# Turning the keys of units 6 and later: one whole-tile stream transpose and 16 transfers inside SBUF in place of 16 small transposes

## The chip, the cores and the metric

The kernel runs on one core of a Trainium2 chip. The metric is the device time of one launch in microseconds; the figure of a kernel is the median of several launches. A core has five engines that each work through a queue of their own in order: TensorE (PE, with its weight loads shown apart as PEld), VectorE (DVE), ScalarE (ACT), GpSimd (POOL) and SyncE (SP). SP computes nothing here: it issues nearly all the DMAs.

## The reference

Two blocks follow each other. The first is a gated linear recurrence over 4 batches, 8 heads, 768 steps, head width 48; the second is a maxout feed-forward network on the 3072 tokens that come out, 384 features wide, with 768 inner features.

```python
f = 1.0 / (1.0 + np.exp(-f_logit))
for t in range(S):
    state = f[:, :, t, :, None] * state + np.einsum('bhd,bhe->bhde', k[:, :, t], v[:, :, t])
    y[:, :, t] = np.einsum('bhd,bhde->bhe', q[:, :, t], state)
x = y.transpose(0, 2, 1, 3).reshape(B * S, H * D)
h = np.maximum(np.maximum(x @ w1, x @ w2), x @ w3)
out = h @ w_out
```

## The kernel before, in words

The recurrence is done in chunks of 64 steps (`C`). A **unit** is one chunk of two batches: 128 token rows (`UT`), eight heads of 48 features padded to 64 (`DP`). There are 24 units (`NU`), numbered `u`; two neighbouring units are the two batch pairs of the same chunk. Four units (`GRP`) make a group of 512 tokens on which the feed-forward network runs. All arithmetic is fp32.

For each unit the kernel makes `kh`, the keys scaled by what the gates leave of them until the chunk's end, and `qh`, the scaled queries, both with features on the partitions (two heads stacked, 2 x 64) and tokens along the row. `pairs(u)` multiplies keys with queries inside the chunk, `values(u)` and `finish(u)` make the outputs, and `sums(u)` (line 437) makes the chunk's contribution to the state: 16 matrix products whose stationary operand is the keys with **tokens** on the partitions, `ks`, and whose moving operand is the values. So `kh` has to be turned into `ks`.

Units 0 to 5 (`BY_ROWS` is 6) are turned on TensorE (`keys`, lines 371 and 373). Units 6 to 21 are turned on VectorE by `keys_by_blocks` (line 386): 16 stream transposes a unit, each of a 32-partition strip with 4 blocks of 32x32. They are issued in four portions of four, two at the end of one pass of the main loop and two in the next.

The rest of a unit's chain, in VectorE's order: `scan(n)` turns the gates (line 300) and runs a scan over them (`r`, line 333); `after(n)` turns the loaded keys into the tile `kt` (line 300, one buffer) and POOL multiplies them with `r` into `kh` (line 344); `before(n)` runs the second scan (`prod`, line 351), turns the queries into `qt` and POOL makes `qh` (line 355).

The order of all instructions is the order in which the code is written (`tc.manual_schedule()`); the framework adds the waits. The main loop runs over `u`. In one pass, with `n = u + 1`, the products of the feed-forward network stand in five portions (`fill(part)`), each a fifth of a unit's share of TensorE work. Between them stand, in this order: `values(u - 1)` and `sums(u - 1)`, `pairs(u)`, `finish(u - 1)`; `pack` (line 528), two DMAs inside SBUF that close up a group's features, in passes where `u % 4` is 3 or 0; loads; `scan(n)`; [portion] `after(n)`, `before(n)`; [portion] `carry(n)`; [portion] the turning of unit `n`'s keys; [portion] `check_load` (line 273), one weight piece loaded again for a check on its range.

SP's queue therefore holds, in the order of the code: loads of `f`, `k`, `q` by `load` (line 187, eight DMAs for each of the three for two units together), of `v` by `load_v` (line 164, two a unit), moves of weights inside SBUF by `place` (lines 462 and 469), `pack`, `check_load`, and the stores of finished tokens (line 564, eight a group). Each DMA signals one of eight semaphores in turn (`DMAHW0` to `DMAHW7`) and waits until the DMA before it on the same one has landed.

Of the kernel before, what the change touches and what calls it, by code (L numbers as in the profile page):

```python
# [9 lines left out]
FP32 = mybir.dt.float32  # L10
# [36 lines left out]
C = 64  # L47
DP = 64
# [7 lines left out]
def kernel(  # L56
# [12 lines left out]
    nc = tc.nc  # L69
    B, H, S, D = q.shape  # L70
    HP = H // 2
    NU = B // 2 * (S // C)
    UT = 2 * C
# [16 lines left out]
    def fast():  # L90
        ctx = ExitStack()
        with ctx:
            work = ctx.enter_context(tc.tile_pool(name="work", bufs=2))
# [57 lines left out]
            BY_ROWS = 6  # L151
# [40 lines left out]
            def load_v(u, queues=one):  # L192
                load_tokens(v_tiles[u % NLD], v, u, queues)
# [109 lines left out]
            ready = {}  # L303
# [24 lines left out]
            def scan(u):  # L328
                gate = gate_tiles[u % 2]
                if u >= BY_ROWS:  # L330
                    turned(gate[:, :, 1:], ready[u])
                r = r_tiles[u % 2]
                nc.vector.tensor_tensor_scan(r[:, 0:LEN][:, ::-1], flat(gate)[:, ::-1], flat(from_one)[:, ::-1], 1.0,  # L333
                                             op0=ALU.mult, op1=ALU.max)
                whole = r[:, 0:LEN].rearrange("p (x t) -> p x t", t=C + 1)[:, :, 1]
                nc.vector.reciprocal(from_inv[u % 2][:, :, 0], whole)
# [28 lines left out]
            def keys(u):  # L365

                if u < min(BY_ROWS, NU - 2):
                    kh = ready[u]["kh"]
                    tr_s = ps_tr.tile([UT, HP, 128], FP32, name="tr")
                    for hp in range(HP):  # L370
                        nc.tensor.transpose(tr_s[:, hp, :], kh[:, hp].rearrange("p a t -> p (a t)"), ident)
                    ks = work.tile([UT, H, DP], FP32, name="ks")
                    nc.scalar.copy(ks.rearrange("s h d -> s (h d)"), tr_s.rearrange("s a d -> s (a d)"))
                    ready[u]["ks"] = ks

            def keys_by_blocks(u, n):

                if BY_ROWS <= u < NU - 2:
                    kh = ready[u]["kh"]
                    if n == 0:  # L380
                        ready[u]["ks"] = work.tile([UT, H, DP], FP32, name="ks")
                    ks = ready[u]["ks"].rearrange("s (hp par) d -> s hp par d", par=2)
                    a, t0 = divmod(n * 32, C)
                    for p0 in range(0, 128, 32):
                        par, e0 = divmod(p0, DP)
                        nc.vector.transpose(ks[n * 32:(n + 1) * 32, :, par, e0:e0 + 32], kh[p0:p0 + 32, :, a, t0:t0 + 32])  # L386

            FOUR = [(par, a) for a in range(2) for par in range(2)]

            def room_of_pairs():  # L390
                return ps_a.tile([128, 2, 512], FP32, name="a")
# [36 lines left out]
            def sums(u, p=None):  # L428

                d, v_ld = ready[u], v_tiles[u % NLD]  # L430
                if u < NU - 2:
                    d["sums"] = y = room_of_pairs() if p is None else p
                    Y = HP * C
                    for hp in range(HP):
                        for par, a in FOUR:
                            s = slice(a * C, (a + 1) * C)
                            nc.tensor.matmul(y[par * DP:(par + 1) * DP, a, Y + hp * D:Y + (hp + 1) * D],  # L437
                                             lhsT=d["ks"][s, 2 * hp + par, :], rhs=v_ld[s, 2 * hp + par, 0:D],
                                             start=True, stop=True)
                    if p is None:  # L440
                        new_state(u)

            def new_state(u):

                d = ready[u]
                if u < NU - 2:
                    ds = d["sums"][:, :, HP * C:HP * (C + D)]
                    new = states[u % 2].rearrange("p (a h) d -> p a (h d)", a=2)
                    if u < 2:
                        nc.scalar.copy(new, ds)  # L450
                    else:
                        nc.vector.tensor_tensor(new, ds, d["state"].rearrange("p (a h) d -> p a (h d)", a=2), op=ALU.add)
# [70 lines left out]
            def pack(u0, u1, xT, queues=one):  # L523

                t = slice(u0 * UT, (u1 + 1) * UT)
                for par in range(2):
                    p0 = par * DP
                    queues[par].dma_start(out=xT[p0 + D:p0 + DP, 0:NK, t], in_=xT[p0:p0 + D, NK, t])
# [447 lines left out]
            def fill(ns):  # L976
                budget[0] += ns
                while budget[0] > 0 and pending:
                    try:
                        budget[0] -= next(pending[0])  # L980
                    except StopIteration:
                        pending.pop(0)
# [18 lines left out]
            with tc.manual_schedule():  # L1001
# [80 lines left out]
                for u in range(GRP, NU):  # L1082
                    n = u + 1
                    part = EARLY if u < BY_ROWS else LATER if u < 2 * GRP else PART
                    if n == BY_ROWS:
                        scan(n)
                    fill(part)
                    keys_by_blocks(u, 2)
                    room_of_unit = room_of_pairs()
                    if u > GRP:  # L1090
                        values(u - 1)
                        sums(u - 1, room_of_unit)
                    keys(u)
                    pairs(u, room_of_unit)
                    if u > GRP:
                        finish(u - 1, xT)
                        if u % GRP == 3:
                            pack(0, 2, xT)
                        elif u % GRP == 0:
                            pack(3, 3, xT)  # L1100
                    if u % GRP == 0:
                        if u > GRP:
                            packed[u // GRP - 1] = xT
                            pending.append(ffn(u // GRP - 1, xT))
                        xT = x_tiles[u // GRP % 2]

                    if u + 2 <= BY_ROWS:
                        load(u + 2)
                    if u == BY_ROWS:
                        load(u + 2, one, "f")  # L1110
                    elif u + 1 != BY_ROWS and BY_ROWS <= u + 3 < NU and u % 2:
                        load(u + 3, one, "fkq" if u % GRP == 1 else "f")
                    if u + 2 < NU:
                        load_v(u + 2)
                    keys_by_blocks(u, 3)
                    if n < NU:
                        if n < BY_ROWS or n == BY_ROWS + 2:
                            sigmoids(n)
                        if n != BY_ROWS:
                            scan(n)  # L1120
                    fill(part)
                    if n < NU:
                        after(n)
                        before(n)
                    if u == 2 * GRP:
                        mix_in(2, nc.vector)
                    check_range(u - CHECKS, 0)
                    fill(part)
                    if BY_ROWS < u + 2 < NU and u % GRP == 0:
                        load(u + 2, one, "k")  # L1130
                    if u == BY_ROWS:
                        load(u + 2, one, "kq")
                    if n < NU:
                        carry(n)
                    else:
                        values(u)
                    check_range(u - CHECKS, 1)
                    fill(part)
                    if BY_ROWS < u + 2 < NU and u % GRP == 0:
                        load(u + 2, one, "q")  # L1140
                    if u == 2 * GRP:
                        for part_of in range(2 * NK + 2):
                            place(w_lin, w_nat, part_of)
                    if n == NU:
                        finish(u, xT)
                        pack(3, 3, xT, both)
                        packed[u // GRP] = xT
                    keys_by_blocks(n, 0)
                    fill(part - 1000 if u < 2 * GRP else part)
                    keys_by_blocks(n, 1)  # L1150
                    check_range(u - CHECKS, 2)
                    if u + 2 >= CHECKS:
                        check_load(u + 2 - CHECKS)
                    if BY_ROWS <= u + 2 < NU and u != BY_ROWS:
                        sigmoids(u + 2)
# [269 lines left out]
```

## Time and profile before

| | |
|---|---|
| device time, median of 3 (lowest, highest) | 406.77 us (406.07, 406.93) |
| span of the profiled execution | 403.7 us |
| PE / PEld busy | 390.9 us (97%) / 339.7 us (84%) |
| DVE busy | 297.7 us (74%) |
| POOL / ACT busy | 256.4 us (64%) / 180.9 us (45%) |
| DMA, mean | 117 GB/s, 181611 packets |
| SP's DMA issues | 423 |

The page of the profile gives each engine's busy time; issuing a DMA is not counted as busy, so SP has no row among them, and its work is read from the timeline of its own queue and from its waits. The profile has no other time for this execution than the span; the median of the launches lies 3.1 us above it. In the rows of groups, the numbers after the bar are busy time, mean duration in ns and the idle time of the engine ahead of them.

### The profile page before, as it was taken

Reading aid. Unit: us, or ns where it says so; the run is one execution under the profiler, and the core shown is the slowest. Engines: PE = TensorE matmul, PEld = TensorE weight load, DVE = VectorE, ACT = ScalarE, POOL = GpSimd, SP = SyncE. Lnnn points to the kernel's source line nnn. Section 1 sums busy time; section 2 is a strip of 40 time slices with the busy share of each in tenths; the row PEclk is TensorE's granted clock in tenths of the full one; section 3 lists DMA queues with packets and bytes.
Section 4 is the critical chain, followed back from the end, with each engine's and each line's share of the span. In section 5 each row is a group of like instructions: output and inputs, shape, how many; then the busy total and the mean of one; then the engine's idle time right before and its main releaser. Section 6 shows DMA issues by size and latency. Waiting matters only on the chain.

```text
span 403.7 us, 11683 instructions
## 1 busy us (share of the span) xinstructions
PE 390.9 (97%) x4658; PEld 339.7 (84%) x4658; DVE 297.7 (74%) x572; ACT 180.9 (45%) x431; POOL 256.4 (64%) x283
## 2 busy tenths in 40 slices
PE   5988999999999999999999999999999999999995
PEld 4766765559998889998889988899988889988995
DVE  6997897999989999897998997998995450002600
ACT  3478787422224442345532344523354425586120
POOL 2189695879997697296587277667477850435700
PEclk9999999999999999999999999999999999999999
DMA  8999986767574576576635477634573003541002
GB/s 171 233 282 284 279 214 89 153 92 150 82 96 114 69 154 135 104 120 84 131 104 97 62 113 88 156 78 81 75 157 91 1 19 87 143 136 70 2 19 63
DMA packets 181611, 47.21 MB, mean 117 GB/s; under 512 B 160497, under 2 KB 179249, under 8 KB 181553
## 3 DMA queue, kind: packets, MB, share of 16 engines
q1 hardware_dynamic: 177536, 45.52, 54.7%
q10 hardware_dynamic: 4016, 0.91, 1.1%
q8 instruction: 37, 0.61, 0.6%
q14 instruction: 22, 0.17, 0.1%
HBM read 37.75 MB, written 4.72 MB: 105 GB/s over the span
## 4 chain that ended last, share of the span: by engine, by line
PE 90%; SPq 4%; DMA 1%; ACT 1%; issue 1%; POOL 1%; DVE 0%
PE p L884 20%; PE p L633 18%; PE tr L884 16%; PE tr L633 14%; PE p L546 7%; PE y L419 3%; PE p L787 3%; PE a L400 2%; PE y L508 2%; PE a L437 2%; SPq L178 2%; DMA v_ld<-in_v_dram 1%; SPq L164 1%; SPq L222 1%; PE tr L295 1%
## 5 line engine op out<-in xcount | busy, mean ns | idle before, releaser
L386 DVE STREAM_TRANSPOSE ks<-kh 32x128 f32<-32x128 f32 x256 | 77.5, 303 | 11.5 <-POOL kh L344 7.4
L884 PE MATMUL tr<-xT,placed 128*128 128x256 f32 x180 | 44.4, 384 | 0.0
L343 POOL COPY ends<-r 128x8 f32<-128x8 f32 x24 | 8.6, 358 | 48.1 <-DVE r L333 48.1
L884 PEld LDWEIGHTS tr<-xT,placed 128*128 128x128 f32 x180 | 33.5, 190 | 4.9
L344 POOL TENSOR_TENSOR kh<-kt,r 128x512 f32<-128x512 f32 x18 | 31.9, 1772 | 8.5 <-DVE kt L300 8.5
L333 DVE TENSOR_TENSOR_SCAN r<-gate,from_one 128x520 f32<-128x520 f32 x24 | 33.2, 1382 | 5.4 <-ACT gate L312 2.8
L546 PE MATMUL p<-xT,w_in 128*128 128x256 f32 (+1 forms) x108 | 33.9, 458 | 3.0 <-POOL w_in L756 1.9
L597 POOL TENSOR_TENSOR w_in<-hm 128x256 f32<-128x256 f32 x18 | 13.3, 737 | 32.2 <-DVE hm L935 29.4
L515 ACT COPY xT<-y 64x256 f32<-64x256 f32 (+1 forms) x60 | 22.1, 368 | 22.4 <-PE y L508 21.7
L351 DVE TENSOR_TENSOR_SCAN prod<-gate,from_inv 128x520 f32<-128x520 f32 x24 | 31.6, 1317 | 0.0
L884 PE MATMUL tr<-xT,w_in 128*128 128x256 f32 x120 | 30.8, 379 | 0.0
L641 DVE TENSOR_TENSOR o<-tr,w_in 128x384 f32<-128x384 f32 (+1 forms) x11 | 5.7, 521 | 33.4 <-PE tr L633 29.0
L884 PE MATMUL p<-w_in,placed 128*128 128x256 f32 x120 | 30.4, 382 | 0.0
L633 PE MATMUL p<-placed,hm 128*128 128x192 f32 x144 | 29.7, 333 | 0.0
L546 PEld LDWEIGHTS p<-xT,w_in 128*128 128x128 f32 x108 | 19.5, 190 | 12.0 <-issue 6.0
L884 PE MATMUL p<-xT,placed 128*128 128x256 f32 x120 | 29.2, 379 | 0.0
L633 PE MATMUL tr<-w_out,w_in 128*128 128x192 f32 x144 | 28.6, 326 | 0.0
L927 DVE TENSOR_TENSOR hm<-tr,hm 128x512 f32<-128x512 f32 x15 | 10.3, 684 | 22.8 <-PE tr L884 15.9
L262 POOL TENSOR_TENSOR w_in<-top_bits,rest_bits 128x384 uint32<-128x384 uint32 x18 | 21.7, 1216 | 7.2 <-DVE top_bits L256 4.3
L884 PEld LDWEIGHTS p<-w_in,placed 128*128 128x128 f32 x120 | 22.4, 190 | 4.4 <-issue 1.5
L638 ACT COPY w_in<-p 128x384 f32<-128x384 f32 x15 | 7.2, 479 | 41.0 <-PE p L633 41.0
L284 ACT ACTIVATE raw<-top_bits 128x384 f32<-128x384 f32 x48 | 25.2, 526 | 0.4
(168 smaller groups left out, 995.6 us busy)
## 6 DMA issues: line engine op xcount, KB each, us to landing
raw<-in_moe_w_dram SPq DMA_DIRECT2D x24, 384.0 KB, 4.4
v_ld<-in_v_dram SPq DMA_DIRECT2D x48, 96.0 KB, 3.4
placed<-in_moe_w_dram SPq DMA_DIRECT2D x12, 384.0 KB, 6.3
out_dram<-o SPq DMA_DIRECT2D x45, 96.0 KB, 2.2
placed<-in_moe_w_out_dram SPq DMA_DIRECT2D x6, 384.0 KB, 5.4
f_ld<-in_f_logit_dram SPq DMA_DIRECT2D x36, 64.0 KB, 2.7
k_ld<-in_k_dram SPq DMA_DIRECT2D x36, 64.0 KB, 2.5
q_ld<-in_q_dram SPq DMA_DIRECT2D x36, 64.0 KB, 2.6
```

Of the source, the lines that this page charges most:

```text
L262: nc.gpsimd.tensor_tensor(dst, by(top), by(rest), op=ALU.add)
L284: nc.scalar.activation(over, size, AF.Relu, scale=(-1 / HI_MIN, 1.0)[step - 1], bias=(1.0, -HI_END * (1 - 2.0 ** -24))[step - 1], accum_ou ...
L333: nc.vector.tensor_tensor_scan(r[:, 0:LEN][:, ::-1], flat(gate)[:, ::-1], flat(from_one)[:, ::-1], 1.0, op0=ALU.mult, op1=ALU.max)
L344: (nc.vector if u < BY_ROWS else nc.gpsimd).tensor_tensor(kh.rearrange("p h a t -> p a h t"), kt, by_batch(r[:, 1:LEN + 1].rearrange("p (x ...
L351: nc.vector.tensor_tensor_scan(flat(prod), flat(gate_tiles[u % 2]), flat(from_inv[u % 2]), 1.0, op0=ALU.mult, op1=ALU.max)
L386: nc.vector.transpose(ks[n * 32:(n + 1) * 32, :, par, e0:e0 + 32], kh[p0:p0 + 32, :, a, t0:t0 + 32])
L419: nc.tensor.matmul(y[o:o + DP, a, hp * C:(hp + 1) * C], lhsT=v_ld[s, 2 * hp + par, :], rhs=d["at"][s, par, hp, :], start=(hp == 0), stop=F ...
L515: nc.scalar.copy(xT[o, :, t0 + a * C:t0 + (a + 1) * C], y[i, a, 0:HP * C].rearrange("p (h t) -> p h t", h=HP))
L546: nc.tensor.matmul(p if w < TOK else p.rearrange("p (two t) -> p two t", two=2), lhsT=w_in[i][:, kt, j * 128:(j + 1) * 128], rhs=x[:, t.st ...
L597: engine.tensor_tensor(dst, x, y, op=op)
L633: nc.tensor.matmul(b[:, p * HD:(p + 1) * HD], lhsT=x, rhs=w, start=id(b) not in begun, stop=True, skip_group_check=True)
L884: nc.tensor.matmul(b[:, j * HALF:(j + 1) * HALF], lhsT=w[:, (2 * n + j) * 128:(2 * n + j + 1) * 128], rhs=x, start=begin and j == 0, stop= ...
```

## The change

`keys_by_blocks` and its four calls a unit go. In their place stands `keys_by_rows`, called once a unit where the first portion stood. It turns the whole of `kh` by one stream transpose of 128 partitions into a tile of 32x32 blocks, whose elements are written 16 bytes apart so that the four head pairs lie innermost, and carries the 16 squares of 32 partitions x 128 elements (512 bytes a row) to their token rows in `ks` by 16 DMAs on SP's queue. The block tile is named `kt` with one buffer, the name and the buffer of the tile that `after` turns the loaded keys into. `sums` reads `ks` through `keys_of`: for units 6 and later a head's 64 features now lie 16 bytes apart.

```diff
-            def keys_by_blocks(u, n):
+            def keys_by_rows(u):
                 if BY_ROWS <= u < NU - 2:
                     kh = ready[u]["kh"]
-                    if n == 0:
-                        ready[u]["ks"] = work.tile([UT, H, DP], FP32, name="ks")
-                    ks = ready[u]["ks"].rearrange("s (hp par) d -> s hp par d", par=2)
-                    a, t0 = divmod(n * 32, C)
-                    for p0 in range(0, 128, 32):
-                        par, e0 = divmod(p0, DP)
-                        nc.vector.transpose(ks[n * 32:(n + 1) * 32, :, par, e0:e0 + 32], kh[p0:p0 + 32, :, a, t0:t0 + 32])
+                    by_32 = work.tile([128, HP * UT], FP32, name="kt", bufs=1)
+                    nc.vector.transpose(by_32.rearrange("p (n d h) -> p n h d", h=HP, d=32),
+                                        kh.rearrange("p h a (n t) -> p (a n) h t", t=32))
+                    ready[u]["ks"] = ks = work.tile([UT, H * DP], FP32, name="ks")
+                    for p in range(4):
+                        for n in range(4):
+                            nc.sync.dma_start(out=ks[n * 32:(n + 1) * 32, p * UT:(p + 1) * UT],
+                                              in_=by_32[p * 32:(p + 1) * 32, n * UT:(n + 1) * UT])
+
+            def keys_of(u, h):
+                ks = ready[u]["ks"]
+                if u < BY_ROWS:
+                    return lambda s: ks[s, h, :]
+                by_32 = ks.rearrange("s (par d hp) -> s par hp d", par=2, hp=HP)
+                return lambda s: by_32[s, h % 2, h // 2, :]
...
-                                             lhsT=d["ks"][s, 2 * hp + par, :], rhs=v_ld[s, 2 * hp + par, 0:D],
+                                             lhsT=keys_of(u, 2 * hp + par)(s), rhs=v_ld[s, 2 * hp + par, 0:D],
...
-                    keys_by_blocks(u, 2)
...
-                    keys_by_blocks(u, 3)
...
-                    keys_by_blocks(n, 0)
+                    keys_by_rows(n)
                     fill(part - 1000 if u < 2 * GRP else part)
-                    keys_by_blocks(n, 1)
```

SP's queue at units 6 and 7, before: the loads of values for two units, then the first move of weights (`placed`, here its first and last rows of a run), then the next loads.

```order
L164 DMA v_ld_128<-in_v_dram 64x8x48 x2
L164 DMA v_ld_129<-in_v_dram 64x8x48 x2
L462 DMA placed_134<-w_in_64 16x3x768 x2
L469 DMA placed_134<-w_in_64 48x768 x2
L469 DMA placed_134<-w_in_64 32x768
L469 DMA placed_134<-w_in_64 16x768
```

The same place in the changed program, whose line numbers are 8 higher from `keys_of` on.

```order
L164 DMA v_ld_128<-in_v_dram 64x8x48 x2
L164 DMA v_ld_129<-in_v_dram 64x8x48 x2
L386 DMA ks<-kt 32x128 x16
L470 DMA placed_134<-w_in_64 16x3x768 x2
L477 DMA placed_134<-w_in_64 48x768 x2
L477 DMA placed_134<-w_in_64 32x768
```

The 16 DMAs of unit 6 stand ahead of the move of weights and of every load behind it; 15 more such blocks follow, one in each unit up to 21.

DVE's queue from the turning of unit 7's keys to that of unit 8's, before (`at` and `st` belong to `pairs` and the state of earlier units, `gate` to the gates of the next); the rows are printed with what each waits for.

```order
L300 STREAM_TRANSPOSE kt<-k_ld_117 128x512
L351 SCALAR_TENSOR_TENSOR prod<-gate_100,from_inv_97 128x520 [waits DVE_49]
L300 STREAM_TRANSPOSE qt<-q_ld_119 128x512 [waits Pool_49]
L386 STREAM_TRANSPOSE ks<-kh 32x4x32 [waits Pool_49]
L386 STREAM_TRANSPOSE ks<-kh 32x4x32 x11
L403 TENSOR_TENSOR at<-a,mask 128x512 [waits PE_49]
L452 TENSOR_TENSOR st_141<-a,state 128x384
L386 STREAM_TRANSPOSE ks<-kh 32x4x32 x4
L300 STREAM_TRANSPOSE gate_99<-sig 128x8x64 [waits Activation_49]
```

The same stretch in the changed program.

```order
L300 STREAM_TRANSPOSE kt<-k_ld_117 128x512 [waits DMAHW4_49,DMAHW5_49,DMAHW3_49,DMAHW6_49,DMAHW2_49,DMAHW7_49,DMAHW1_49,DMAHW0_49]
L351 SCALAR_TENSOR_TENSOR prod<-gate_100,from_inv_97 128x520 [waits DVE_49]
L300 STREAM_TRANSPOSE qt<-q_ld_119 128x512 [waits Pool_49]
L381 STREAM_TRANSPOSE kt<-kh 128x4x4x32 [waits Pool_49]
L411 TENSOR_TENSOR at<-a,mask 128x512 [waits PE_49]
L460 TENSOR_TENSOR st_141<-a,state 128x384
L300 STREAM_TRANSPOSE gate_99<-sig 128x8x64 [waits Activation_49]
```

Sixteen rows of DVE have become one (line 381), and the turning of unit 7's loaded keys into `kt`, which waited for nothing (the loads of the two units of a pair were waited for at the first of them), now waits for the DMA semaphores of all eight lanes.

## The prediction

> **What bounds the kernel now.** I read the page first (busy shares, the chain that ended last), then the busy time of the stretch in which the change works, then SP's waits and SP's issue durations, since that queue has no busy row.
>
> ```profile
> PE 390.9 (97%) x4658; PEld 339.7 (84%) x4658; DVE 297.7 (74%) x572; ACT 180.9 (45%) x431; POOL 256.4 (64%) x283
> PE 90%; SPq 4%; DMA 1%; ACT 1%; issue 1%; POOL 1%; DVE 0%
> 75.00:300.00 225.00, 224.97 (x3027) 200.51 (x3025) 204.83 (x433) 87.30 (x213) 163.63 (x171) 1.00 0.61 106
> ```
>
> The last row is the stretch from 75 to 300 us, in which units 6 to 21 are turned: PE 224.97 of 225.00 us busy, DVE 204.83, ACT 87.30, POOL 163.63, granted clock 1.00. PE is the bound and waits for nothing there; DVE has 0% of the chain. Work taken off DVE can therefore bring PE forward by 0.03 us in this stretch at most.
>
> SP is the queue to which the change adds. Its waits from 75 to 295 us (total, times, longest), the rows of its own queue at both ends of the turning, and its issue durations (ns, lowest/median/highest):
>
> ```profile
> SPq L528 <- ACT xT L515: 31.6, 5, 7.4
> ...
> 70.48 1.32 SPq L462 DMA_DIRECT2D placed<-w_in  x2
> 71.84 5.69 SPq L469 DMA_DIRECT2D placed<-w_in  x8
> ...
> 258.49 0.53 SPq L273 DMA_DIRECT2D raw<-in_moe_w_dram  x1
> 259.12 1.40 SPq L164 DMA_DIRECT2D v_ld<-in_v_dram  x2
> 260.61 0.61 SPq L273 DMA_DIRECT2D raw<-in_moe_w_dram  x1
> ...
> 290.20 4.15 SPq L187 DMA_DIRECT2D q_ld<-in_q_dram  x8
> 294.39 0.49 SPq L273 DMA_DIRECT2D raw<-in_moe_w_dram  x1
> ```
> ```profile
> L469 SPq DMA_DIRECT2D placed<-w_in x16: 587/592/1226, 71.8 to 99.3; - x16
> L469 SPq DMA_DIRECT2D w_in<-w_in x8: 519/588/592, 122.3 to 127.0; - x8
> ...
> DMA to landing us min/median/max: 1.9/2.7/4.2
> ...
> L528 SPq DMA_DIRECT2D xT<-xT x19: 556/613/1336, 99.9 to 334.2; - x19
> ...
> L187 SPq DMA_DIRECT2D f_ld<-in_f_logit_dram x72: 312/487/2723, 50.1 to 272.8; - x72
> ...
> L273 SPq DMA_DIRECT2D raw<-in_moe_w_out_dram x6: 327/330/536, 344.3 to 366.2; - x6
> ```
>
> SP issues one DMA after the other, each for about half a microsecond, and stands still for only 31.6 us of those 220, in five waits for the copies ahead of `pack`. The first block of new DMAs comes in ahead of the row at 70.48, the last ahead of the row at 294.39 (the check load behind unit 21). SP needs 294.39 - 70.48 = 223.9 us for what lies between, 192.3 of them without the five waits.
>
> **The change part by part.** *DVE.* Removed: 256 small transposes, 77.5 us by the first row below. Added: 16 of 128x512 elements; the transposes of that size took 0.684 us, so 10.9 us. No row writes at 16-byte steps; from the same price to twice it, 10.9 to 21.9 us. DVE loses 56 to 67 us of work, which PE, as shown, does not wait for: worth nothing to the end.
>
> ```profile
> L386 DVE STREAM_TRANSPOSE ks<-kh 32x128 f32<-32x128 f32 x256 | 77.5, 303 | 11.5 <-POOL kh L344 7.4
> ...
> L300 DVE STREAM_TRANSPOSE kt<-k_ld x18: 662/684/715, 71.6 to 313.1; 128x512 f32<-128x512 f32 x18
> ...
> L437 PEld LDWEIGHTS a<-v_ld,ks x704: 129/135/136, 14.5 to 308.9; 64*64 64x64 f32 x176
> ...
> 308.02 0.69 PE L419 MATMUL y<-at,v_ld 64*64 64x64 f32 x32
> 308.54 0.63 PE L437 MATMUL a<-v_ld,ks 64*64 64x48 f32 x32
> 308.99 0.66 PE L400 MATMUL a<-qh,kh 48*64 48x64 f32 x32
> ```
>
> *PE.* Count and order are the same. What is new is the 16-byte step of the stationary operand in `sums`. The 32 products of `sums(21)` take 308.99 - 308.54 = 0.45 us from their start to that of the next group. Lower bound: nothing, since a strided read has no way to be faster than a contiguous one. Upper: weight loads at half pace double the block, 16 x 0.45 = 7.2 us. I take 0, because PE will have slack (below). [...] No run so far shows a strided weight load.
>
> *SP.* 16 x 16 = 256 more issues. The nearest rows are moves inside SBUF with one contiguous run a partition: 0.588 and 0.592 us, the same for 16, 32 and 48 partitions (one row holds all three). The `pack` rows, partly of the same 512-byte runs, say 0.613. Between two issues lie 0.04 us ((4.15 - 0.49) / 7 = 0.52 us a load against 0.487). I take 0.59 + 0.04 = 0.63 us: 10.1 us a unit, 161 us in all. The idle 31.6 us take up a fifth of that. The bounds are the cheapest DMA of this queue, 0.33 + 0.04 = 0.37 us (95 us in all), and the loads' 0.53 us (135 us).
>
> *The waits.* The 16 DMAs wait for DVE's transpose, hence for POOL's `kh`, hence for the `kt` of the same unit; the next unit's `kt` waits until the 16 have landed, since both tiles have one buffer. Behind that wait stand all later DVE instructions: the second scan, the queries, and what empties PE's accumulators. So once SP is late, DVE stops in front of `kt`, PE a little later for want of a free accumulator, and everything moves at SP's pace. On SP itself all loads, packs and stores queue behind the 16. Does SP then ever wait in turn? The loop from the last issue of one block to the first of the next is landing (1.9 us at least), then from `kt` to the turning of `kh`, which the rows below show as 259.85 - 256.96 = 2.9 us, then 0.7 us for the transpose: 5.5 to 6.3 us. SP has more than that to issue between nearly all blocks. Only ahead of units 15 and 19 has it just one check load and two loads of values (258.49 to 260.52, 2.0 us): about 4 us of waiting each, 8 us.
>
> ```profile
> 256.96 0.67 DVE L300 STREAM_TRANSPOSE kt<-k_ld 128x512 f32<-128x512 f32 x1
> 257.55 1.20 DVE L351 TENSOR_TENSOR_SCAN prod<-gate,from_inv 128x520 f32<-128x520 f32 x1
> ...
> 259.85 1.22 DVE L386 STREAM_TRANSPOSE ks<-kh 32x128 f32<-32x128 f32 x4
> ...
> 300.26 0.71 DVE L300 STREAM_TRANSPOSE kt<-k_ld 128x512 f32<-128x512 f32 x1 [0.17 <-DMA out_dram<-o]
> ...
> 75.39 1.24 DVE L386 STREAM_TRANSPOSE ks<-kh 32x128 f32<-32x128 f32 x4
> ```
>
> *The sum.* Unit 6's keys can be issued at 75.4 + 0.7 = 76.1 us. From there SP works without a break: 76.1 + 192.3 + 161 + 8 = 437.4 us until unit 21's last issue, 439.3 when it has landed. What waits for it is `kt` of unit 22, at 300.26 before, or, if PE has run ahead to it, `sums(21)` at 308.54. The rest of the program is as it was, and its DMAs are few. The end moves by 439.3 - 300.3 = 139.0 or by 439.3 - 308.5 = 130.8 us; the middle is 135, so the span becomes 403.7 + 135 = 539 us. The median lies 3.1 us above the span now (406.77 against 403.7), so I predict 542 us. `pack` costs nothing more: when SP reaches it, the copies that it waited 31.6 us for lie far back.
>
> **The rivals.** *The issues are hidden, no change.* From the last SP wait to PE there is room for 31.6 us; if an issue of these small regular DMAs took no more than 31.6 / 256 = 0.12 us, SP would never be late. Then PE stays the bound and the time is 406.8 us, or 414 with the dear weight loads. For it: DVE is relieved of 56 us or more, and nothing on PE changes its place. Against it: of SP's rows above none has a lowest value under 0.31 us. [...] Here the rows have 0.59 us against 2.7 us to landing, a fifth, and the issues of one queue add up while the landings overlap.
>
> *The issues are cheap but not hidden.* At 0.37 us the sum falls by 66 us to 476, at the loads' 0.53 by 26 to 516. For it: one plain contiguous load has the low price. Against it: its source is in HBM; every row with a source in SBUF is near 0.6.
>
> *PE loses its clock while it waits.* At the start of the program the same four transposes take twice as long as 7 us later:
>
> ```profile
> 4.40 1.08 PE L295 MATMUL tr<-ident,f_ld 128*128 128x128 f32 x4 [4.40 <-DVE q_ld L148]
> ...
> 9.29 1.05 PE L295 MATMUL p<-ident,k_ld 128*128 128x128 f32 x4
> ...
> 11.39 0.60 PE L295 MATMUL tr<-ident,f_ld 128*128 128x128 f32 x4
> ```
>
> So after idle time PE runs at half pace for about 6.5 us, a loss of 3.3 us. From block to block a unit will last (437.4 - 76.1 - 10.1) / 15 = 23.4 us; now it lasts (300.3 - 71.6) / 16 = 14.3 us from `kt` to `kt`, all of it PE work. So PE idles some 9 us a unit and may pay this each time. SP covers it where it has much to issue; if it were paid on the path after all 15 waits, 50 us: 592 us.
>
> **How the numbers follow.** Forecast (SP paces units 6 to 21, 490 to 590 us): 0.84. Cheap issues, below 490: 0.07. Clock lost on the path, above 590: 0.05. Hidden issues or a change that moves nothing: 0.04, of which 0.01 faster, 0.02 within 0.2% (about what a measurement of this kernel can tell from no change), 0.01 slower through the weight loads. The range runs from between the two cheaper prices to the full clock loss. Slower in all: 0.97.
>
> **What would show it.** In the profile after: 256 issues of `ks<-kt` with a median near 0.59 us; SP without its five waits ahead of `pack`; `kt` in the page's groups with long idle time ended by a DMA of `ks`; PE's share near 73% (391 of 539); DVE's busy time near 235 us; the chain that ended last on SP and DMA for most of 75 to 440 us; from unit 22 on the same 95 to 103 us as before. Wrong would be: issues under 0.4 us; `ks` landing much later than 2 us, or `kt` released early while PE still waits (then it is not the shared buffer that paces DVE); rows of `sums` spread to 0.9 us or more.

## The result, and the profile after

The changed kernel takes 551.07 us (median of 4 runs, 549.24 to 552.79) against 406.42 us for the kernel before (405.59 to 406.93): the ratio is 1.356, 95% interval 1.352 to 1.360. The profiled execution has a span of 548.5 us. The forecast was 542 us, and slower.

First the page of the changed kernel: the busy rows, the granted clock, the chain that ended last by engine and by line, and two of the costliest groups (at their right: busy time, mean ns of one, idle time ahead of them and what ended it).

```profile
PE 439.4 (80%) x4658; PEld 380.0 (69%) x4658; DVE 243.0 (44%) x332; ACT 180.4 (33%) x431; POOL 265.0 (48%) x283
PEclk9999999866867795999696799978589988999999
SPq 43%; PE 37%; issue 5%; DVE 4%; DMA 4%; POOL 3%; ACT 2%; DVEq 0%; ACTq 0%; POOLq 0%
SPq L386 21%; SPq L187 14%; PE p L641 9%; PE p L892 7%; PE tr L641 6%; PE tr L892 5%; PE p L554 3%; SPq L477 3%; SPq L164 2%; DMA ks<-kt 2%; SPq L572 2%; PE a L408 1%; POOL kh L344 1%; PE y L516 1%; POOL qh L355 1%
L300 DVE STREAM_TRANSPOSE kt<-k_ld 128x512 f32<-128x512 f32 x18 | 12.8, 709 | 181.9 <-DMA ks<-kt 181.9
L344 POOL TENSOR_TENSOR kh<-kt,r 128x512 f32<-128x512 f32 x18 | 34.7, 1926 | 169.0 <-DVE kt L300 169.0
```

PE's part of the chain fell from 90% to 37%, SP's queue has 43% instead of 4%, and half of that is the new line L386. `kt` stands 181.9 us in front of the buffer that the transfers of the unit before still read; POOL's `kh` stands behind it.

Next the rows of the new transfers and of the new transpose (ns, lowest/median/highest), the landing, SP's one notable wait between 75 and 447 us, pieces of SP's timeline, and the busy time by stretches (PE, PEld, DVE, ACT, POOL, then the granted clock):

```profile
L386 SPq DMA_DIRECT2D ks<-kt x256: 517/589/1785, 77.7 to 445.9; - x128
...
DMA to landing us min/median/max: 1.7/1.8/3.7
...
L381 DVE STREAM_TRANSPOSE kt<-kh x16: 1073/1096/1176, 76.4 to 427.1; 128x512 f32<-128x512 f32 x16
...
SPq L386 <- DVE kt L381: 12.6, 3, 5.6
...
377.01 11.19 SPq L386 DMA_DIRECT2D ks<-kt  x16
388.30 0.53 SPq L273 DMA_DIRECT2D raw<-in_moe_w_dram  x1
388.87 1.39 SPq L164 DMA_DIRECT2D v_ld<-in_v_dram  x2
393.79 10.48 SPq L386 DMA_DIRECT2D ks<-kt  x16
...
436.37 10.09 SPq L386 DMA_DIRECT2D ks<-kt  x16
...
75.00:300.00 225.00, 163.32 (x1773) 140.83 (x1771) 84.50 (x108) 49.96 (x120) 104.38 (x102) 0.82 0.44 78
300.00:447.00 147.00, 117.41 (x1330) 106.02 (x1330) 66.47 (x87) 42.52 (x106) 68.70 (x70) 0.88 0.38 70
447.00:549.00 102.00, 93.76 (x711) 85.55 (x710) 30.72 (x48) 39.18 (x103) 46.43 (x49) 0.96 0.28 75
```

The five waits ahead of `pack` (31.6 us before) are gone; SP issues without a break but for the waits for a transpose, one of which stands between 390.3 and 393.8. A block of 16 transfers takes 10.1 to 11.3 us of the queue. In the stretch from 75 to 300 us PE is busy for 163 of 225 us instead of all 225, at a granted clock of 0.82 instead of 1.00.

At the end of the stretch the last landing lets go both of what the prediction named (start, duration in us; in brackets the idle time before and what ended it):

```profile
447.71 1.12 PE L445 MATMUL a<-v_ld,ks 64*64 64x48 f32 x26 [0.65 <-DMA ks<-kt]
447.80 0.71 DVE L300 STREAM_TRANSPOSE kt<-k_ld 128x512 f32<-128x512 f32 x1 [13.57 <-DMA ks<-kt]
```

`sums(21)` and `kt` of unit 22 start within 0.1 us of each other.

### The profile page after: what moved, and what is told of

It reads as the page before. It is cut to its first block, busy times and chain, and to the rows that moved or that the text cites. A ratio compares the mean times of both kernels' runs of the same rounds, so it can differ in the third digit from the quotient of the medians.

```text
span 548.5 us, 11770 instructions
## 1 busy us (share of the span) xinstructions
PE 439.4 (80%) x4658; PEld 380.0 (69%) x4658; DVE 243.0 (44%) x332; ACT 180.4 (33%) x431; POOL 265.0 (48%) x283
## 4 chain that ended last, share of the span: by engine, by line
SPq 43%; PE 37%; issue 5%; DVE 4%; DMA 4%; POOL 3%; ACT 2%; DVEq 0%; ACTq 0%; POOLq 0%
SPq L386 21%; SPq L187 14%; PE p L641 9%; PE p L892 7%; PE tr L641 6%; PE tr L892 5%; PE p L554 3%; SPq L477 3%; SPq L164 2%; DMA ks<-kt 2%; SPq L572 2%; PE a L408 1%; POOL kh L344 1%; PE y L516 1%; POOL qh L355 1%
## 5 line engine op out<-in xcount | busy, mean ns | idle before, releaser
L300 DVE STREAM_TRANSPOSE kt<-k_ld 128x512 f32<-128x512 f32 x18 | 12.8, 709 | 181.9 <-DMA ks<-kt 181.9
L445 PE MATMUL a<-v_ld,ks 64*64 64x48 f32 x704 | 35.9, 276 | 54.6 <-DMA ks<-kt 52.7
L445 PEld LDWEIGHTS a<-v_ld,ks 64*64 64x64 f32 x704 | 31.7, 188 | 57.8 <-DMA ks<-kt 32.5
L892 PE MATMUL tr<-xT,placed 128*128 128x256 f32 x180 | 51.8, 432 | 0.0
L408 PE MATMUL a<-qh,kh 48*64 48x64 f32 x768 | 21.4, 258 | 29.4 <-POOL qh L355 28.7
L892 PEld LDWEIGHTS tr<-xT,placed 128*128 128x128 f32 x180 | 38.7, 220 | 7.1
L408 PEld LDWEIGHTS a<-qh,kh 48*64 48x64 f32 x768 | 18.1, 166 | 32.0 <-POOL qh L355 30.2
L333 DVE TENSOR_TENSOR_SCAN r<-gate,from_one 128x520 f32<-128x520 f32 x24 | 36.3, 1511 | 5.6 <-ACT gate L312 3.0
L927 ACT COPY top_bits<-p 128x512 f32<-128x512 f32 x15 | 8.8, 585 | 72.5 <-DVE hm L943 61.3
L641 PEld LDWEIGHTS p<-placed,hm 128*128 128x128 f32 x144 | 24.6, 195 | 1.4 <-ACT w_in L646 1.1
```

Of the source, the lines that this page charges most:

```text
L408: nc.tensor.matmul(p[t, par, hp * C:(hp + 1) * C], lhsT=kh[r, hp, a, :], rhs=qh[r, a, hp, :], start=True, stop=True)
L641: nc.tensor.matmul(b[:, p * HD:(p + 1) * HD], lhsT=x, rhs=w, start=id(b) not in begun, stop=True, skip_group_check=True)
L892: nc.tensor.matmul(b[:, j * HALF:(j + 1) * HALF], lhsT=w[:, (2 * n + j) * 128:(2 * n + j + 1) * 128], rhs=x, start=begin and j == 0, stop= ...
```

## The experiments

Theory 1 (T1), the mechanism of the prediction: the time of SP's queue for 256 more issues is the loss. T2 and T3 are the rivals of one experiment each and are named in its expectation. Against T1 stand: the work that the change gives DVE and PE, the bytes and rows of the transfers, and the waits that tie DVE, SP and PE together through the one buffer. Ratios are to the kernel before on the same chip, whose median was 405.7 to 406.6 us in these comparisons.

### Idle transfers in the kernel before

```diff
+            idle_to = keep.tile([128, 128], FP32, name="idle_to")
+            def idle_transfers(u):
+                if BY_ROWS <= u < NU - 2:
+                    for p in range(4):
+                        for n in range(4):            # idle4: range(1)
+                            nc.sync.dma_start(out=idle_to[n * 32:(n + 1) * 32, :], in_=ident[p * 32:(p + 1) * 32, :])
...
                     keys_by_blocks(n, 0)
+                    idle_transfers(n)
```

> The kernel before, unchanged in its turning of keys, with 16 idle transfers a unit (32 partitions x 512 bytes inside SBUF, from a constant to a tile that nobody reads) on SP's queue at the place of the changed kernel's 16. Theory 1, SP's issue time paces the program: 15 blocks of 10.1 us stand ahead of the last loads of queries, whose last issue ends at 294.4 us now, 31.6 us of them waits that vanish; 294.4 - 31.6 + 151.9 = 414.7, 2.6 us to landing, needed at 302.0: the end moves by 115 us, to about 521 us (512 to 535). Theory 2, what paces it is that keys arrive by DMA and that their tile shares a buffer with the turned loads: nothing of that is here, 406 to 412 us.

> The same with 4 idle transfers a unit. Theory 1: 4 x 16 x 0.63 = 40 us against the 31.6 us in which SP stands still: SP falls behind by at most some 9 us and has the lead of its loads to spend first, so 406 to 416 us, most likely 409. A cost that goes with the number of transfers instead of with the queue being full would be a quarter of that of 16, about 29 us: 435.

With 16 a unit: 529.85 us, ratio 1.307 (1.302 to 1.311). With 4: 416.33 us, 1.025 (1.022 to 1.029). SP's rows for the idle transfers, first with 16, then with 4 a unit:

```profile
L395 SPq DMA_DIRECT2D idle_to<-ident x256: 507/588/1912, 71.0 to 432.6; - x128
```
```profile
L395 SPq DMA_DIRECT2D idle_to<-ident x64: 575/589/1879, 70.9 to 314.2; - x64
```

Transfers that nobody waits for, and that wait for no transpose, cost 123 us when there are 256 of them. What is late is what SP issues anyway, as the longest waits of the kernel with 16 show (total us, times, longest):

```profile
ACT top_bits L282 <- DMA raw<-in_moe_w_dram: 105.2, 13, 18.9
...
POOL xT L878 <- DMA xT<-xT: 57.8, 4, 15.8
```

From 64 to 256 issues the time rises by 113.5 us, 0.59 us an issue: past the idle time of SP, each issue costs about its own duration. By the mean of the 256 (0.636 us, and 0.04 us between two) it would be 0.68 us; but the moves and loads among them were issued in 165 us instead of 180, for a reason that is not known. The first 64 cost 9.9 us, just above the 416 us expected at most. They used up SP's idle time: the waits ahead of `pack` are 0.9 us instead of 31.6. By their mean (0.653 us) they are 44 us of issues and not 40, the moves and loads among them took 180 us instead of 176, and the check load behind unit 21 goes out at 314.8 us instead of 294.4. About half of these 20 us reaches the end.

### The change without its transfers

In `none_contig` the sums read a constant tile, contiguously, and the transpose writes contiguously; `none_step16` keeps the 16-byte step of both; `own_none` is `none_contig` with the memory plan (which tile has how many buffers) of the kernel `own_tile` below.

```diff
-                    ready[u]["ks"] = ks = work.tile([UT, H * DP], FP32, name="ks")
-                    for p in range(4):
-                        for n in range(4):
-                            nc.sync.dma_start(...)
+                    ready[u]["ks"] = from_one.rearrange("p x t -> p (x t)")[:, 0:H * DP]
```

> The changed kernel without its 16 transfers a unit: the whole-tile transpose stays on VectorE with a contiguous write, and the score matmuls of units 6 to 21 read a constant tile of zeros and ones, contiguously, in place of the keys (left out: the carrying of the keys, so the sums are of a constant). What is left of the change is one transpose in place of 16 small ones. T1 (SyncE's issues are the loss): the time is that of before, 406.4 us, within 1 per cent (404 to 410). T2 (much of the loss is in other parts of the change, the order of VectorE or the one buffer that is shared): 430 or more. T3 (relief of VectorE is worth something once the issues are gone): below 403.

> As none_contig, with the transpose's write and the score matmuls' stationary operand at the 16-byte step of the changed kernel. T1 (the step costs TensorE's loads 0.45 us a unit, from the sums block's 1.45 us against 1.00 with contiguous weights, and SyncE is the rest): 16 x 0.45 = 7 us over none_contig, 413 to 415, on the path, because TensorE bounds the kernel again. T2 (the step's loads hide behind the matmuls in flight when TensorE is not waiting): within 1 us of none_contig. Bound above, if the whole of 1.45 - 0.41 = 1.04 us came from the step: 17 us, 423.

> none_contig with the memory plan of own_tile: a tile of two buffers for the transpose's result, one buffer each for the gates' sigmoids and the products of the state; no transfers (left out: the keys in the sums). T1 (own_tile began its first block 6.5 us later because of the single buffers, and gave there what it took at the end): 410 to 416. T2 (the single buffers cost nothing, the late start is from elsewhere): 404 to 408.

`none_contig`: 405.76 us, ratio 1.0005 (0.998 to 1.003). `none_step16`: 413.34 us, 1.017 (1.012 to 1.022). `own_none`: 413.82 us, 1.018 (1.012 to 1.024). The page of `none_contig`, its busy row:

```profile
PE 390.4 (97%) x4658; PEld 340.3 (84%) x4658; DVE 229.5 (57%) x332; ACT 181.3 (45%) x431; POOL 261.5 (65%) x283
```

DVE has 68 us less work than before (297.7) and the time is the same: the relief is worth nothing. The step of 16 bytes costs 7.6 us. The weight loads of `none_step16`, strided and (units 0 to 5) contiguous, show why:

```profile
L441 PEld LDWEIGHTS a<-v_ld,from_one x512: 190/213/213, 91.2 to 316.1; 64*64 64x64 f32 x171
...
L441 PEld LDWEIGHTS a<-v_ld,ks x192: 129/135/135, 14.5 to 79.3; 64*64 64x64 f32 x192
```

`own_none` costs 7 to 8 us over `none_contig` (8.1 by the medians, 7 by the ratios): the single buffers of that plan are not free, which matters for the next two sections.

### The shared buffer, and the step, in the changed kernel

`own_tile` gives the transpose a tile `by_32` of its own with two buffers, in place of the shared `kt`; to make room, the gates' sigmoids and the products of the state get one buffer each. `contig` puts the heads outermost again, so that the transpose writes and the sums read contiguously, and the transfers write runs of 128 bytes.

```diff
-                    by_32 = work.tile([128, HP * UT], FP32, name="kt", bufs=1)     # own_tile
+                    by_32 = work.tile([128, HP * UT], FP32, name="by_32")
```
```diff
-                            nc.sync.dma_start(out=ks[n * 32:(n + 1) * 32, p * UT:(p + 1) * UT],     # contig
-                                              in_=by_32[p * 32:(p + 1) * 32, n * UT:(n + 1) * UT])
+                            nc.sync.dma_start(out=to[n * 32:(n + 1) * 32, p // 2, p % 2],
+                                              in_=by_32[...].rearrange("i (h d) -> i h d", h=HP))
```

> The changed kernel with a tile of its own, of two buffers, for the turned blocks (two other tiles go from two buffers to one to make room), so that the next unit's loaded keys can be turned while the 16 transfers run. Theory 1: the 256 issues stay, only SP's three waits for the transpose (12.6 us) go and about 3 us at the end, where the queries no longer wait for the landing: 551 - 16 = 535 us (528 to 543). Theory 2, the shared buffer paces it (DVE waits 181.9 us there): a large part of that comes back, below 500 us.

> The changed kernel with the heads outermost in the block tile: the transpose writes and the products read contiguous elements, and the 16 transfers write runs of 128 bytes instead of 512. Theory 1: SP has as much to issue, 548 us (544 to 551), 1 us of it for three shorter transposes ahead of SP's waits. Theory 3, the stationary operand's 16-byte step (1.4 us for the products of a unit instead of 0.42) lies on the path: 16 x 1.0 = 16 us less, 535 us. If 128-byte runs make an issue dearer, it shows in its row and the time goes up by 256 times that.

`own_tile`: 546.88 us, ratio 1.349 (1.343 to 1.355), 12 us above the likeliest value. `contig`: 553.34 us, 1.364 (1.360 to 1.367). In `own_tile`, `kt` waits for no transfer any more; the wait has moved to `sums` and to the emptying of PE's accumulator behind it:

```profile
DVE at L411 <- PE a L408: 123.5, 16, 16.4
...
PE a L445 <- DMA ks<-by: 79.9, 25, 8.2
```
```profile
L386 SPq DMA_DIRECT2D ks<-by x256: 517/589/1802, 84.2 to 444.8; - x128
```

So the shared buffer decides who stands still, and by little for how long. The first block goes out at 84.2 instead of 77.7 us. Most of that lateness is there without any transfers: in `own_none`, with the same memory plan, SP's loads in that stretch are 4.5 us behind those of `none_contig` (the value loads at 73.10 and 68.63). The rows give the rest of the account. SP's two waits of 3.5 us between the blocks are gone, and from the last issue's end to the end lie 98.4 us instead of 102.0; against these 10.6 us stand the 6.5 us at the start, which leaves 4.1, and 4.2 were measured. So T1's gain was there, and the late start took more than half of it; and of the 12.6 us of waits that the forecast took off, 5.6 stand ahead of the first block and could not go. `contig` has the contiguous loads' 135 ns back in its rows and gains nothing: in the changed kernel the step is not on the path. Its issues, with runs of 128 bytes, have a median of 0.599 us instead of 0.589.

### Fewer issues, or another queue

`split` (built on `own_tile` and `contig`) issues 8 of the 16 transfers from ScalarE's queue. `by_hbm` (built on `own_tile`) carries the tile by one store to HBM and 4 loads. `four` is the changed kernel with 4 transfers a unit.

```diff
-                            nc.sync.dma_start(out=to[...], in_=by_32[...])     # split
+                            (nc.sync, nc.scalar)[n % 2].dma_start(out=to[...], in_=by_32[...])
```
```diff
+                    nc.sync.dma_start(out=on_hbm[u % 2], in_=by_32)     # by_hbm; the loads one pass later
+                    for n in range(4):
+                        nc.sync.dma_start(out=ready[u]["ks"][n * 32:(n + 1) * 32, :].rearrange("i (p x) -> i p x", p=4),
+                                          in_=on_hbm[u % 2].rearrange("(p i) (n x) -> n i p x", p=4, n=4)[n])
```
```diff
                     for p in range(4):     # four
-                        for n in range(4):
-                            nc.sync.dma_start(...)
+                        s = slice(p * 32, (p + 1) * 32)
+                        nc.sync.dma_start(out=ks[s, :], in_=by_32[s, :])
```

> The changed kernel with a tile of two buffers for the transpose's result, heads outermost, and 8 of a unit's 16 transfers issued by ScalarE's queue, 8 by SyncE's. T1 (the issuing engine's time is the price): SyncE gets 16 x 8 x 0.63 = 81 us of issues where it stood idle for 32, so about 49 us late, and the sum with 546.9 of own_tile less the 81 us taken off is 466; ScalarE's 81 us go into its idle time in part: 446 to 480, likeliest 462. T2 (the 16 transfers are slow in themselves, or the DMA engines are full of them, whoever issues them): 530 to 550, as own_tile. T3 (ScalarE's queue becomes the pace, since its activations stand behind the waits of its issues): over 480 and below 530.

> The changed kernel with a tile of two buffers for the transpose's result; the 16 transfers a unit inside SBUF are replaced by one store of the tile to a scratch in HBM and 4 loads of 32 rows each from there: 5 issues a unit in place of 16, for the same bytes and the same 512-byte runs. T1 (the number of issues is the price): 16 x 5 x 0.63 = 50 us of issues against 32 us idle, so some 19 us late, as the 4 idle issues a unit gave 10 us, and the step of 16 bytes 0 to 7 us: 416 to 433, likeliest 424. T2 (the bytes or the 512-byte runs are the price): over 520.

> The changed kernel with 4 transfers a unit in place of 16, each of 32 partitions by 512 numbers, the same bytes between the same two tiles (left out: the 16 blocks' change of place, so the sums are of keys in a wrong order). T1 (the number of issues is the price): 413.3 of none_step16, the 10 us that 4 idle transfers a unit gave, and 0 to 9 us for waiting on the landing: 420 to 432, likeliest 425. T2 (the bytes within SBUF, or the wait of sums and turn for the landing, are the price): 520 or more.

`split`: 507.55 us, ratio 1.250 (1.243 to 1.257). `by_hbm`: 455.26 us, 1.116 (1.107 to 1.125). `four`: 454.40 us, 1.116 (1.113 to 1.119). All three move the way T1 says and none comes down as far as it says. Where the rest lies is read from the waits of each.

`split`, ScalarE's issues and ACT's own waits between 75 and 450 us:

```profile
L387 ACTq DMA_DIRECT2D ks<-by x128: 592/612/876, 83.6 to 389.2; - x128
```
```profile
ACT raw L284 <- DMA ks<-by: 30.3, 3, 11.1
...
ACT o L728 <- DMA ks<-by: 26.8, 4, 13.2
ACT top_bits L699 <- DMA ks<-by: 23.1, 3, 7.8
```

ScalarE issues at SP's price (0.612 us, SP's half 0.600), and its activations stand behind the eight issues of a unit and behind what these wait for (the idle times in the rows contain the issues): the case called T3.

`by_hbm`, SP's waits in the same stretch: the loads wait for the store's landing, and everything behind them in the queue waits too. The memory plan of `own_tile`, with its 7 to 8 us, comes on top.

```profile
SPq L393 <- DMA hbm<-by: 26.8, 14, 3.3
```

`four` carries all bytes, and each of its issues costs what an issue of a quarter of the bytes costs (0.588 against 0.589 us). The bytes are the same in both, so they are not what makes the difference. From `four` to the changed kernel lie 192 issues and 96.7 us, 0.50 us for each. But it stands 41 us above `none_step16`, where 4 idle transfers a unit cost 9.9. Its waits, DVE's over the whole span and SP's between 75 and 350 us, and SP's timeline around unit 9, whose keys are turned at 129.2 us:

```profile
DVE kt L300 <- DMA ks<-kt: 56.1, 7, 13.5
```
```profile
SPq L386 <- DVE kt L381: 25.2, 6, 5.4
```
```profile
131.40 5.15 SPq L187 DMA_DIRECT2D q_ld<-in_q_dram  x8
136.91 1.26 SPq L469 DMA_DIRECT2D w_in<-w_in  x2
138.22 5.03 SPq L476 DMA_DIRECT2D w_in<-w_in  x8
143.36 3.11 SPq L386 DMA_DIRECT2D ks<-kt  x4
```

The block goes out 14 us after its transpose, since the loads and moves ahead of it in the queue come first; at other units SP stands at the block until DVE has turned the keys. Each side loses by waiting for the other's turn. Between its first and its last block (77.7 to 346.1 us) SP waits 19.8 us for the transposes and 15.4 us for the copies ahead of `pack`; in the kernel with 4 idle transfers a unit it is none and 0.9 us, and the check load behind unit 21 goes out at 314.8 us instead of 346.1. That these waits, about 35 us, are the remaining 30 us is read from the traces; no kernel with another order in the queue was run. In the changed kernel SP stands still for 8.6 us in all between its first and its last issue; that is why the 192 issues more cost 0.50 us each, and not the 0.66 us of their mean duration (0.616) and the 0.04 us between two.

### The parts added up again

`step16_idle` is `none_step16` with 16 idle transfers a unit out of a constant; `step16_from_kt` reads them from the transpose's result.

```diff
                     ready[u]["ks"] = from_one.rearrange("p x t -> p (x t)")[:, 0:H * DP]
+                    for p in range(4):
+                        for n in range(4):
+                            nc.sync.dma_start(out=idle_to[n * 32:(n + 1) * 32, :],
+                                              in_=ident[p * 32:(p + 1) * 32, :])     # step16_idle
+                                              in_=by_32[p * 32:(p + 1) * 32, n * UT:(n + 1) * UT])     # step16_from_kt
```

> none_step16 (the changed kernel without its transfers, the sums reading a constant tile at the 16-byte step) with the 16 idle transfers a unit of idle16, read from a constant at the place where the changed kernel has its own: nobody waits for them and they wait for nobody (left out: the carrying of the keys). T1 (where SyncE is the pace, the step's 7.6 us lie beside it): 529 to 534, as idle16. T2 (the parts add up): 537 to 540.

> step16_idle with the 16 transfers read from the transpose's result, so that SyncE waits for each unit's transpose and the next turn of the keys waits for the last landing, as in the changed kernel; only the sums wait for no landing, since the tile that is written is read by nobody (left out: the keys in the sums). T1 (the pace is SyncE, and its waits for the transposes are most of the rest): 541 to 549 of the changed kernel's 551. T2 (TensorE's waits for the landing are what makes up the rest): 529 to 536.

`step16_idle`: 529.67 us, ratio 1.304 (1.300 to 1.310), the same as `idle16`. `step16_from_kt`: 552.79 us, 1.361 (1.356 to 1.365), the same as the changed kernel. Their transfer rows:

```profile
L388 SPq DMA_DIRECT2D idle_to<-ident x256: 507/588/1944, 69.8 to 433.8; - x128
```
```profile
L388 SPq DMA_DIRECT2D idle_to<-kt x256: 507/588/1537, 76.7 to 445.8; - x128
```

The sum of the change closes: 123 us for SP's issues, 0 for the step beside them, 23 us for tying the transfers to the transpose, and nothing measurable for the sums' wait on the landing. The 23 us lie in three places of these rows and the spans (526.2 and 549.3 us): the first issue 6.9 us later, 5.1 us more from the first issue to the last (369.1 against 364.0), and 11.1 us more from the last issue to the end (103.5 against 92.4), since now the program's rest begins with that landing.

## Why the prediction was right

The forecast fell 9 us short and its mechanism is the one that the runs show. By its steps:

- *PE bound, DVE's relief worth nothing.* Right: `none_contig`. The sized part was too low: a transpose written at 16-byte steps takes 1.096 us, not the 0.684 taken, within the 0.684 to 1.37 given (21.9 us over 16). DVE's busy time is 243 us, not 235.
- *The issues.* 256 with a median of 0.589 us, as taken. The sum of 161 us was the mis-sized term: the median was used where the mean counts. Ten issues took 0.8 to 1.8 us, 13.2 us together, so that the 16 blocks, 10.1 to 11.3 us each, need 169 us. That is 7.8 of the 9 us.
- *SP's other work and its waits.* Right: between the first and the last issue SP stands still for 8.6 us, 8 forecast. Two waits of 3.5 us make most of it, and they stand ahead of units 15 and 19, where 4 us each were forecast; the third wait of the row above lies ahead of unit 6. The first block came at 77.7, 1.6 us after the 76.1 forecast: the transpose began 1.0 us later than the first small one before (76.4 against 75.4) and takes 0.4 us longer than taken. Together the last issue began at 445.9 and was over at 446.5 instead of 437.4.
- *What waits for it.* Right, and both at once: PE had run ahead to `sums(21)`, and `kt` of unit 22 came with it. From the last issue's end to the end lie 102.0 us, 101.6 in the sum (539 less 437.4). So close a hit is luck: the sum took the middle of two values 8 us apart and did not decide between them.
- *The weight loads.* The price of 0 was right in this kernel and only because PE has slack: where PE is the bound the step costs 7.6 us, just over the upper end of 7.2. The sign given for an error did come, rows of `sums` that spread to more than 0.9 us, and it was no error of the path. The block of `sums` in the changed kernel and in `four`, and PE's wait instructions for these blocks in the two:

```profile
413.41 1.61 PE L445 MATMUL a<-v_ld,ks 64*64 64x48 f32 x31
414.77 0.30 PE L408 MATMUL a<-qh,kh 48*64 48x64 f32 x5
...
L445 PEldq EVENT_SEMAPHORE  x128: 51/51/3204, 92.0 to 446.8; - x128
```
```profile
205.79 1.12 PE L444 MATMUL a<-v_ld,ks 64*64 64x48 f32 x32
206.73 0.66 PE L407 MATMUL a<-qh,kh 48*64 48x64 f32 x32
...
L444 PEldq EVENT_SEMAPHORE  x32: 51/51/682, 92.0 to 357.3; - x32
```

  From start to the next group's start it is 1.36 us in the changed kernel and 0.94 in `four`, both with the step, against 0.45 before. So 0.49 us belong to the step (16 times that is 7.8 us, about what `none_step16` lost) and some 0.4 us to something that 16 transfers bring and 4 do not. It is the products' waits on more landings: in `step16_from_kt`, where the 16 transfers run and the sums wait for none, the block takes 0.93 us, and in `contig`, where they wait without the step, 1.01. PE's weight-load queue has eight wait instructions a unit in the changed kernel and two in `four`; each takes 0.051 us where the landing is long past, 0.41 us for eight. The half pace behind the 7.2 us was the author's assumption; the rows show 213 against 135 ns for a weight load (`none_step16`), and 1.096 us for the new transpose, which writes at the step, against 0.711 us for that of the loaded keys in the same run (L300, 128x512 too), which writes contiguously.
- *The rivals.* Hidden issues fail on `idle16`. In the changed kernel an issue takes 0.589 us against 1.8 us to landing, but the 256 stand one behind the other in SP's queue and hold it for 169 us. Cheap issues fail on the 0.589. The clock did fall, to 0.82 and 0.88, and PE's busy time rose by 48.5 us; that is why PE's share is 80% and not the 73% forecast, which divided the old busy time. Of the 48.5 us, 7.8 are the step (390.4 in `none_contig`, 398.2 in `none_step16`) and 28.5 come in `step16_from_kt` (426.7), whose granted clock is 0.884 and whose sums wait for no transfer of keys; the last 12.7 come with these waits. Up to the last issue the clock was not paid on the path: that time is made of SP's own rows. Behind the landing a little may have been: from 449.2 to 456.1 us the granted clock is 0.51, PE is busy for 4.3 of these 6.9 us (32 products `a` of line 408 take 1.14 us after 2.97 us of idle time, against 0.66 us in the row at 308.99 before), and half of that 4.3, an estimate of 2 us at most, could be the loss.

Of the other signs, the chain on SP's queue came as told (43%; of the 37% of PE, about 203 us, 76 us lie between 75 and 447 us and the rest before and after). The shared buffer was the place of the wait but not its cause: `own_tile` moved the wait and kept nearly all of the time.

## What to carry to other kernels

Ask of each DMA how long its issuing queue is held, not only how long it flies: here 0.59 us of SP for each issue inside SBUF, whether it carried 512 bytes or 2 KB a partition, against 31.6 us of idle time in all. Sum such a queue by means, not medians, and where it paces the kernel count first what it issues (16 to 4 a unit gave back 97 us), then how its order meets the waits of the engine that feeds it. Work taken off an engine that the bound never waits for is worth nothing, here 68 us of it.

## What the runs showed that was not expected

Four dependent transfers a unit cost 41 us over `none_step16`, four idle ones 9.9 us over the kernel before: on a queue that issues in order, a transfer that waits for another engine, and is waited for by it, cost 0.64 us here, four times the 0.15 us of one that stands alone. ScalarE's queue issues no cheaper than SP's (0.612 against 0.600 us in `split`). And one buffer instead of two for two tiles that no part of the change touches cost 7 to 8 us (`own_none`), as much as the whole step of 16 bytes.
